# The handover between two layers: residual tiles in a pool of their own, and a piece of a weight moved behind them

## The chip, the cores and the metric

One NeuronCore of a Trainium2 chip runs the whole program. The metric is the device time of one execution in microseconds (us); lower is better. Most figures below come from a profiled execution, whose span is within a few us of its timed value.

## The reference

The program runs two kinds of layer, each twice, with a residual around each: A, B, A, B.

```python
x = A_x                                                       # [1, 2048, 640], bf16
x = x + _A_ref(_layernorm(x), A_wq, A_wk, A_wv, A_wo, A_beta)
x = x + _B_ref(_layernorm(x), B_mem0, B_Wq, B_Wk, B_Wv, B_Wo, B_seg_len)
x = x + _A_ref(_layernorm(x), A_wq, A_wk, A_wv, A_wo, A_beta)
x = x + _B_ref(_layernorm(x), B_mem0, B_Wq, B_Wk, B_Wv, B_Wo, B_seg_len)
```

A is an attention with a compressive memory over 4 segments of 512 rows (32 heads of 20). It ends with `o @ wo` and the residual. B is a recurrence: 64 segments of 32 rows, each attending to itself and to 8 memory rows that the segment before it produced (32 heads of 128). So B's steps are serial, and each ends with the product by `Wo` (32 heads, each 128 x 640 in bf16, 160 KB).

```python
for s in range(n_seg):                                        # layer B
    h = jnp.concatenate([mem, x[:, s*32:(s+1)*32]], axis=1)
    ...                                                       # q, k, v, masked softmax, o
    o = jnp.einsum('bhte,hed->btd', o, Wo)
    mem = o[:, :M, :].copy()
```

## The kernel before

Layer A works in row blocks of 128. In the last segment its output projection `outp` is deferred: layer B calls it as the list `tail`, between B's first products. Each row block takes two products `a_YP` of 320 columns, VectorE's addition of the residual `a_xr`, a store of the float32 rows, a cast to bf16 on GpSimd into `a_xb`, and a store of that. There is one `a_xb` buffer (pool `so`) and there are two `a_xr` buffers (pool `so2`), so the residual tiles of blocks 2 and 3 can only be loaded when blocks 0 and 1 are through.

```python
def res_load(n, tt, q=nc_raw.sync):
    r0 = n * 512 + tt * 128
    xr = so2.tile([128, D], xdt, name="a_xr")
    q.dma_start(xr[:], x_src[r0:r0 + 128, :])
    xin[tt] = xr

def outp(n, i):
    tt, half = divmod(i, 2)
    if half == 0:
        xin[tt, "o"] = so2.tile([128, D], F32, name="a_xo") if src_is_bf16 else xin[tt]
    xo = xin[tt, "o"]
    hs = slice(320 * half, 320 * half + 320)
    YP = pg.tile([128, 320], F32, name="a_YP", tag="pg")
    for c in range(NCH):
        nc.tensor.matmul(YP[:], lhsT=oT[:, c, 128 * tt:128 * tt + 128], rhs=wvo[:, c, hs], ...)
    nc.vector.tensor_tensor(out=xo[:, hs], in0=YP[:], in1=xin[tt][:, hs], op=ALU.add)
    if half:
        r0 = n * 512 + tt * 128
        nc_raw.sync.dma_start(x_dst[r0:r0 + 128, :], xo[:])
        xb = so.tile([128, D], BF16, name="a_xb")
        nc.gpsimd.tensor_copy(xb[:], xo[:])
        nc_raw.sync.dma_start(xb_dst[r0:r0 + 128, :], xb[:])
        if tt + 2 < 4:
            res_load(n, tt + 2, nc.scalar if n == NS - 1 else nc_raw.sync)
```

Wo fills memory as it comes free: heads 0 to 10 while A still runs, heads 11 to 15 by five loads on ScalarE's queue during B's first products, heads 16 to 31 once A's pools are closed.

```python
wo = [wop.tile([128, NW1 - NEARLY, D], BF16, name="b_wo1")]     # NW1 = 16, NEARLY = 11
# ... cut ...
for kind in ("Q", "K", "V"):
    for b in range(2):
        TailUnit(0, kind, b).run(NCH)                           # b_tail in the trace
        flush()
        h = NEARLY + {"K": 0, "V": 2}.get(kind, NW1) + b
        if h < NW1:
            nc.scalar.dma_start(wo[0][:, h - NEARLY, :], wo_src[:, h, :])
for Wt, dst in ((W.wq, QT), (W.wk, KT)):
    for b in range(2):
        # ... cut: one more such load ...
        tail(2)                                                 # two a_YP products of A
        # ... cut: b_first, placed by ScalarE and GpSimd ...
tail(100)
tails_to_seg(0)
outer.close()                                                   # A's pools end here
wop2 = ctx.enter_context(tc.tile_pool(name="b_wo2", bufs=1, side="right", reuse_waits="tile"))
wo.append(wop2.tile([128, 32 - NW1, D], BF16, name="b_wo2"))
for a, b in ((NW1, 24), (24, 32)):
    nc_raw.sync.dma_start(wo[1][:, a - NW1:b - NW1, :], wo_src[:, a:b, :])
```

A scheduler then orders the instructions of each engine. A load waits until the last user of the memory that it takes is done.

Of the kernel before, what the change touches and what calls it, by code (L numbers as in the profile page):

```python
# [18 lines left out]
F32 = mybir.dt.float32  # L19
BF16 = mybir.dt.bfloat16  # L20
# [3 lines left out]
PSUM = bass.MemoryType.PSUM  # L24

S_TOK = 2048
NW1 = 16
EARLY = [(tag, h0, n, at) for tag, h0, n in (("a_phiks", 0, 1), ("a_MZ32", 1, 2), ("a_xnT0", 3, 4), ("a_vaug0", 7, 4)) for at in range(n)]
NEARLY = len(EARLY)
ORDER_ENGINES = ("tensor", "scalar", "vector", "gpsimd")  # L30
D = 640
# [169 lines left out]
def layer_A(nc, nc_raw, tc, C, W, A_wv, A_wo, x_src, x_dst, xb_dst, src_is_bf16, general, outer, mem0, wo_src, prep=None, prefetch=()):  # L201

    SC = 1.0 / math.sqrt(20.0)
    NS, NG = 4, 8
    NU = NS * NG
    xdt = BF16 if src_is_bf16 else F32
    with ExitStack() as ctx:
        br = Bridge()
# [32 lines left out]
        def wload(u):  # L241
            if prep and u < NG:
                wts[u] = W.pad[u]
                return
            wt = wk.tile([128, 2, NCH, 128], BF16, name="a_wt")
            for k in range(2):
                nc_raw.sync.dma_start(wt[:, k].rearrange("p c m -> p (c m)"), W.wpad[u % NG][k])
            wts[u] = [wt[:, 0], wt[:, 1]]
# [78 lines left out]
        def run(gctx):  # L327
# [13 lines left out]
            us, xin = {}, {}  # L341
# [15 lines left out]
            def phi_q(u):  # L357
                if u // NG == 0:
                    return
                U = us[u]  # L360
                t1 = wk1.tile([128, 512], BF16, name="a_t1q", tag="t1")
                nc.vector.tensor_scalar(out=t1[:], in0=U.qk[:, 0, :], scalar1=1.0, scalar2=1.0, op0=ALU.add, op1=ALU.max)
                nc.vector.tensor_tensor(out=U.phiq[:], in0=U.phiq[:], in1=t1[:], op=ALU.min)
# [15 lines left out]
            def row_max(u):  # L379

                U = us[u]
                negm = gp.tile([128, 4, 4], F32, name="a_negm")
                for j in range(4):
                    for qc in range(4):
                        N = 128 * (qc + 1)
                        Sx = pss.tile([128, 2, 512], F32, name="a_Sg", tag="pss")
                        nc.tensor.matmul(Sx[:, 0, 0:N], lhsT=U.qk[32 * j:32 * j + 32, 0, 128 * qc:128 * qc + 128],
                                         rhs=U.qk[32 * j:32 * j + 32, 1, 0:N], start=True, stop=False, tile_position=(32 * j, 0))
                        nc.tensor.matmul(Sx[:, 0, N - 128:N], lhsT=C.identb[:], rhs=negu[:], start=False, stop=True)
                        nc.vector.tensor_reduce(out=negm[:, qc, j:j + 1], in_=Sx[:, 0, 0:N], axis=AX.X, op=ALU.max, negate=True)  # L390
                parts = gp.tile([128, 4, 4, 3], BF16, name="a_mparts")
                for i in range(3):
                    nc.vector.tensor_copy(parts[:, :, :, i], negm[:])
                    if i < 2:
                        nc.vector.tensor_tensor(out=negm[:], in0=negm[:], in1=parts[:, :, :, i], op=ALU.subtract)
                mt = pg.tile([12, 4, 128], BF16, name="a_mt", tag="pg")
                for qc in range(4):
                    nc.tensor.transpose(mt[:, qc, :], parts[:, qc].rearrange("p j i -> p (j i)"), C.identb[:])
                ms = wk1.tile([12, 512], BF16, name="a_ms", tag="t1")
                nc.vector.tensor_copy(ms[:], mt[:].rearrange("p q t -> p (q t)"))  # L400
                for j in range(4):
                    nc_raw.sync.dma_start(U.qk[32 * j + 20:32 * j + 23, 0, :], ms[3 * j:3 * j + 3, :])
                    nc_raw.sync.dma_start(U.qk[32 * j + 20:32 * j + 23, 1, :], ones[:])
# [93 lines left out]
            def o_turn(tt):  # L497
                nc_raw.sync.dma_start(oT[:, :, 128 * tt:128 * tt + 128], Onat[:, tt, :], transpose=True)

            def res_load(n, tt, q=nc_raw.sync):  # L500
                r0 = n * 512 + tt * 128
                xr = so2.tile([128, D], xdt, name="a_xr")
                q.dma_start(xr[:], x_src[r0:r0 + 128, :])
                xin[tt] = xr

            def outp(n, i):
                tt, half = divmod(i, 2)
                if half == 0:
                    xin[tt, "o"] = so2.tile([128, D], F32, name="a_xo") if src_is_bf16 else xin[tt]
                xo = xin[tt, "o"]  # L510
                hs = slice(320 * half, 320 * half + 320)
                YP = pg.tile([128, 320], F32, name="a_YP", tag="pg")
                for c in range(NCH):
                    nc.tensor.matmul(YP[:], lhsT=oT[:, c, 128 * tt:128 * tt + 128], rhs=wvo[:, c, hs], start=(c == 0), stop=(c == NCH - 1))
# [4 lines that stand above are left out]
                    xb = so.tile([128, D], BF16, name="a_xb")  # L519
                    nc.gpsimd.tensor_copy(xb[:], xo[:])  # L520
                    nc_raw.sync.dma_start(xb_dst[r0:r0 + 128, :], xb[:])
                    if tt + 2 < 4:
                        res_load(n, tt + 2, nc.scalar if n == NS - 1 else nc_raw.sync)

            ln = {}

# [85 lines left out]
            for u in range(NU + 1):  # L612
                more = u + 1 < NU
                if u + 2 < NU:
                    wload(u + 2)
                if pre and u % 2:
                    pre.pop(0)()
                if fill_pads and u + 2 < NG:
                    fill_pads(nc, u + 2)
                for slot in range(6):  # L620
                    if u < NU:
                        score(u, slot)
                    if slot == 0 and more:
                        proj(u + 1, 0)
                    if slot == 1 and u >= 1:
                        pvmm(u - 1, 1)
                        norm(u - 1)
                    if slot == 2 and more:
                        proj(u + 1, 1)
                        phi_q(u + 1)  # L630
                    if slot == 4 and u < NU:
                        pvmm(u, 0)
                        if more:
                            phi_k(u + 1)
                    if slot == 5 and u < NU:
                        nummm(u)
                        memory(u)
                    extras(u, slot)
                if general and more:
                    row_max(u + 1)  # L640
            br.tail = [lambda i=i: outp(NS - 1, i) for i in range(8)]

        with ExitStack() as gctx:
            run(gctx)
# [24 lines left out]
def layer_B(nc, nc_raw, tc, C, W, br, outer, wo_src, x_src, xb_src, x_dst, general, nsteps=64, out_bf16=False):  # L669
# [4 lines left out]
    with ExitStack() as ctx:  # L674
# [5 lines left out]
        wop = ctx.enter_context(tc.tile_pool(name="b_wo", bufs=1, reuse_waits="tile"))  # L680
        wo = [wop.tile([128, NW1 - NEARLY, D], BF16, name="b_wo1")]
        pp = ctx.enter_context(tc.tile_pool(name="b_ps", bufs=3, reuse_waits="tile", space=PSUM))

        def wo_of(h):
            for t, h0, n in br.wo:
                if h0 <= h < h0 + n:
                    return t[:, h - h0]
            return wo[0][:, h - NEARLY] if h < NW1 else wo[1][:, h - NW1]

        def ps_tile(shape, dtype, name):  # L690
            return pp.tile(shape, dtype, name=name, tag="ps")
# [43 lines left out]
        def heads(t):  # L735
            return t[:].rearrange("p (h c) -> p h c", h=32)
# [94 lines left out]
        def flush():  # L831
            while done:
                done.pop(0)()

        def tails_to_seg(s):
            T, i = divmod(s, 4)
            nc.gpsimd.tensor_copy(heads(QT[s])[:, :, 32:40], QTt[T][:, :, 8 * i:8 * i + 8])
# [67 lines left out]
        for kind in ("Q", "K", "V"):  # L905
            for b in range(2):
                TailUnit(0, kind, b).run(NCH)
# [6 lines that stand above are left out]
                h = NEARLY + 4 + (b if Wt is W.wq else NW1)  # L914
                if h < NW1:
                    nc.scalar.dma_start(wo[0][:, h - NEARLY, :], wo_src[:, h, :])
# [3 lines left out]
                place(("act", "pool")[b], turn(ps[:]), b, heads(dst[0]), 0, 24, 0)  # L920
        tail(100)
        tails_to_seg(0)
        outer.close()
        wop2 = ctx.enter_context(tc.tile_pool(name="b_wo2", bufs=1, side="right", reuse_waits="tile"))
        wo.append(wop2.tile([128, 32 - NW1, D], BF16, name="b_wo2"))
        for a, b in ((NW1, 24), (24, 32)):
            nc_raw.sync.dma_start(wo[1][:, a - NW1:b - NW1, :], wo_src[:, a:b, :])
        po = ctx.enter_context(tc.tile_pool(name="b_po", bufs=1, reuse_waits="tile", space=PSUM))
        pot = ctx.enter_context(tc.tile_pool(name="b_pot", bufs=2, reuse_waits="tile", space=PSUM))

# [374 lines left out]
```

## Time and profile before

| | before |
|---|---|
| time, median of 4 runs (range) | 2270.47 us (2269.4 to 2272.89) |
| span of the profiled run | 2272.9 us |
| TensorE busy | 2156.6 us, 95% |
| first handover, idle of TensorE in it | 58.31 us, 11.45 us |
| second handover, idle of TensorE in it | 61.80 us, 11.63 us |

The unit for everything that follows is the length of a handover: from TensorE's first `b_tail` matmul, when all of A's products but the deferred `a_YP` are out, to its first `b_Qa` matmul of B's third step. Both ends are read from TensorE's timeline. The table of stretches then gives the work inside, here for the two handovers of the kernel before (columns: the stretch and its length, then busy time and count of TensorE, its weight loads, VectorE, ScalarE, GpSimd; granted clock, DMA share, GB/s):

```profile
288.64:346.95 58.31, 46.86 (x955) 23.68 (x956) 28.08 (x64) 10.56 (x29) 19.57 (x44) 0.89 0.47 123
...
1408.20:1470.00 61.80, 50.17 (x959) 24.57 (x960) 27.67 (x64) 10.46 (x29) 19.84 (x44) 0.82 0.43 121
```

Length minus TensorE's busy time is its idle time. TensorE's work is the same in both handovers, so the difference in busy time, 50.17 against 46.86, is clock: 0.82 against 0.89.

### The profile page before, as it was taken

To read this page: it belongs to the slowest core of one execution; us is meant where nothing else is said; L and a number is where in the kernel's file an instruction comes from. 1 tells how busy PE (TensorE), PEld (TensorE's weight loads), DVE (VectorE), ACT (ScalarE), POOL (GpSimd) and SP (SyncE) were. 2 spreads that over 40 slices of the span, in tenths; PEclk is the share of its full clock that TensorE was granted. 3 is DMA by queue.
4 is the path that set the end of the run, shared out by engine and by line. 5 is a ranking of instruction groups with operands and counts; after the bars stand their busy time and mean duration, and the time that the engine had idled before them with its cause. 6 is when DMAs were issued, how large, how long until landed. Compare 5 with 4: busy or idle time off the path is not lost.

```text
span 2272.9 us, 122154 instructions
## 1 busy us (share of the span) xinstructions
PE 2156.6 (95%) x54486; PEld 1213.7 (53%) x54548; DVE 1632.6 (72%) x3998; ACT 908.6 (40%) x2111; POOL 1023.7 (45%) x2475
## 2 busy tenths in 40 slices
PE   6998889999999999999979999799999999999997
PEld 3444445555555555555544444455555555555554
DVE  5787646777777677777668887477777777777775
ACT  5776723332323323333357766233333233333322
POOL 3454434444444444444423545344444444444442
PEclk9999989999999999999989999899999999999999
DMA  6677841101110101000144665310101110010000
GB/s 159 162 177 176 225 124 23 24 21 28 22 23 21 24 22 24 23 23 19 28 112 123 151 167 137 117 24 18 21 19 20 19 22 19 20 24 19 17 13 14
DMA packets 150233, 137.78 MB, mean 61 GB/s; under 512 B 76080, under 2 KB 139584, under 8 KB 147776
## 3 DMA queue, kind: packets, MB, share of 16 engines
q1 hardware_dynamic: 145504, 124.30, 22.2%
q8 instruction: 428, 7.01, 1.3%
q10 hardware_dynamic: 4192, 5.57, 0.9%
q14 instruction: 109, 0.89, 0.1%
HBM read 89.17 MB, written 26.21 MB: 51 GB/s over the span
## 4 chain that ended last, share of the span: by engine, by line
PE 81%; DVE 7%; DMA 5%; ACT 3%; issue 2%; POOL 1%; SPq 1%; DVEq 0%; ACTq 0%; POOLq 0%
PE b_V L87 13%; PE b_OPS L87 13%; PE b_tail L87 10%; PE b_Qa L87 6%; PE b_Kb L87 6%; PE b_Ka L87 6%; PE b_Qb L87 6%; PE b_SP L87 5%; PE b_OTL L87 4%; PE b_OPSd L87 3%; PE a_PP L87 3%; ACT a_PT L87 2%; PE a_S L87 2%; PE a_VP L87 1%; PE a_pv L87 1%
## 5 line engine op out<-in xcount | busy, mean ns | idle before, releaser
L87 PEld LDWEIGHTS <-b_hT 128*32 128x32 bf16 x15120 | 376.1, 96 | 311.4 <-DVE b_hT L87 69.4
L87 ACT ACTIVATE b_PT<-b_SP 128x224 bf16<-128x224 f32 x256 | 92.2, 360 | 764.2 <-PE b_SP L87 742.5
L87 PE MATMUL b_V<-b_wv,b_hT 128*32 128x512 bf16 x5040 | 358.5, 381 | 0.4 <-issue 0.2
L87 ACT ACTIVATE a_PT<-a_S 128x768 bf16<-128x768 f32 (+1 forms) x384 | 325.9, 883 | 73.1 <-PE a_S L87 51.5
L87 PE MATMUL b_OPS<-b_wo,b_OTsb 128*32 128x320 bf16 x5376 | 258.9, 302 | 8.1 <-DVE b_OTsb L87 5.1
L87 PEld LDWEIGHTS <-b_OTsb 128*32 128x32 bf16 x8192 | 202.0, 97 | 96.3 <-DVE b_OTsb L87 48.2
L87 POOL CAST b_QT<-b_TQ 128x384 bf16<-128x384 f32 x254 | 140.1, 551 | 223.2 <-DVE b_TQ L87 223.2
L87 ACT CAST b_OTsb<-b_OTL 128x320 bf16<-128x320 f32 x384 | 151.2, 427 | 208.2 <-PE b_OTL L87 189.6
L87 POOL TENSOR_TENSOR b_PT<-b_PT,b_R 128x64 bf16<-128x64 bf16 x256 | 105.2, 411 | 215.6 <-ACT b_R L87 198.6
L87 POOL CAST b_KT<-b_TQ 128x384 bf16<-128x384 f32 x254 | 142.4, 561 | 131.6 <-DVE b_TQ L87 128.0
L87 PE MATMUL b_Qa<-b_wq,b_hT 128*32 128x512 bf16 x2520 | 183.6, 384 | 5.0 <-DVE b_hT L87 5.0
L87 PE MATMUL b_Kb<-b_wk,b_hT 128*32 128x512 bf16 x2520 | 183.0, 380 | 0.0
L87 PE MATMUL b_Ka<-b_wk,b_hT 128*32 128x512 bf16 x2520 | 182.9, 383 | 0.0
L87 POOL TENSOR_SCALAR_AFFINE_SELECT a_PT<-a_PT 128x256 bf16<-128x256 bf16 x256 | 109.0, 429 | 157.5 <-ACT a_PT L87 155.3
L87 DVE STREAM_TRANSPOSE b_TM<-b_OPS 128x128 f32<-128x128 f32 x252 | 88.2, 350 | 123.0 <-PE b_OPS L87 119.1
L87 PE MATMUL b_Qb<-b_wq,b_hT 128*32 128x512 bf16 x2520 | 158.4, 379 | 0.0
L87 PE MATMUL a_PP<-a_xnT,a_wt 128*128 128x512 bf16 x505 | 139.3, 388 | 14.6 <-ACT a_phiq L87 5.4
L87 DVE CAST b_Vsb<-b_V 128x512 bf16<-128x512 f32 x128 | 88.5, 692 | 80.0 <-PE b_SP L87 45.6
L87 PE MATMUL b_OPS<-a_wo,b_OTsb 128*32 128x320 bf16 x2816 | 144.6, 301 | 0.0
L87 PE MATMUL a_S<-a_qk 32*128 32x512 bf16 (+3 forms) x1024 | 136.4, 307 | 5.9 <-ACT a_PT L87 4.7
L87 DVE CAST b_OTsb<-b_OTL 128x320 bf16<-128x320 f32 x128 | 62.9, 492 | 100.1 <-PE b_OTL L87 100.1
L87 POOL TENSOR_TENSOR b_Rtot<-b_Rtot,b_R 128x160 bf16<-128x160 bf16 x256 | 126.7, 495 | 0.0
(158 smaller groups left out, 4282.4 us busy)
## 6 DMA issues: line engine op xcount, KB each, us to landing
a_wt<-a_wpad SPq DMA_DIRECT2D x112, 160.0 KB
b_XO<-xres SPq DMA_DIRECT2D x256, 30.0 KB
a_wvo<-in_A_wo_dram SPq DMA_DIRECT2D x8, 800.0 KB
b_wq<-in_B_Wq_dram SPq DMA_DIRECT2D x20, 256.0 KB
b_wk<-in_B_Wk_dram SPq DMA_DIRECT2D x20, 256.0 KB
xres<-a_xo SPq DMA_DIRECT2D x16, 320.0 KB
xres_bf<-a_xb SPq DMA_DIRECT2D x32, 160.0 KB
b_wv<-in_B_Wv_dram SPq DMA_DIRECT2D x20, 256.0 KB
```

The lines of the kernel that those rows point to most:

```text
L87: r = f(*a, **k)
```

## The change

The intent is to let the deferred output projection run without waiting for loads. The residual tiles of row blocks 2 and 3 (and, where the source is bf16, the float32 output tile of block 2) get buffers of their own in a pool `a_tail`, and are loaded ahead of need from SyncE's queue. To make room, Wo's heads 12 to 15 leave the early piece. They are loaded into `a_tail`'s place when it closes, in one 640 KB load ahead of heads 16 to 31.

```diff
-NW1 = 16
+NW1 = 12
@@ res_load, outp
-            def res_load(n, tt, q=nc_raw.sync):
+            def res_load(n, tt):
...
-                q.dma_start(xr[:], x_src[r0:r0 + 128, :])
+                nc_raw.sync.dma_start(xr[:], x_src[r0:r0 + 128, :])
...
-                if half == 0:
+                if half == 0 and (tt, "o") not in xin:
...
-                xo = xin[tt, "o"]
+                xo = xin.pop((tt, "o")) if half else xin[tt, "o"]
...
-                    if tt + 2 < 4:
-                        res_load(n, tt + 2, nc.scalar if n == NS - 1 else nc_raw.sync)
+                    if tt + 2 < 4 and n < NS - 1:
+                        res_load(n, tt + 2)
@@ end of layer A
+            def tail_tiles(pool):
+
+                for tt in (2, 3):
+                    r0 = (NS - 1) * 512 + tt * 128
+                    xin[tt] = pool.tile([128, D], xdt, name=f"a_xr{tt}")
+                    nc_raw.sync.dma_start(xin[tt][:], x_src[r0:r0 + 128, :])
+                if src_is_bf16:
+                    xin[2, "o"] = pool.tile([128, D], F32, name="a_xo2")
+
+            br.tail_tiles = tail_tiles
@@ layer B
+        tail_ctx = ExitStack()
+        br.tail_tiles(tail_ctx.enter_context(tc.tile_pool(name="a_tail", bufs=1, reuse_waits="tile")))
...
+        tail_ctx.close()
         outer.close()
+        wop3 = ctx.enter_context(tc.tile_pool(name="b_wo3", bufs=1, reuse_waits="tile"))
         wop2 = ctx.enter_context(tc.tile_pool(name="b_wo2", bufs=1, side="right", reuse_waits="tile"))
-        wo.append(wop2.tile([128, 32 - NW1, D], BF16, name="b_wo2"))
-        for a, b in ((NW1, 24), (24, 32)):
-            nc_raw.sync.dma_start(wo[1][:, a - NW1:b - NW1, :], wo_src[:, a:b, :])
+        wo.append(wop3.tile([128, 16 - NW1, D], BF16, name="b_wo3"))
+        wo.append(wop2.tile([128, 16, D], BF16, name="b_wo2"))
+        nc_raw.sync.dma_start(wo[1][:], wo_src[:, NW1:16, :])
+        for a, b in ((16, 24), (24, 32)):
+            nc_raw.sync.dma_start(wo[2][:, a - 16:b - 16, :], wo_src[:, a:b, :])
```

## The prediction

> **What bounds the kernel now.** I read the page first, then the table of stretches, then the chain of work that ended last through both handovers, then the timeline of each engine there, last the trace's records of DMA packets, semaphore landings and granted clock. The page:
>
> ```profile
> PE 2156.6 (95%) x54486; PEld 1213.7 (53%) x54548; DVE 1632.6 (72%) x3998; ACT 908.6 (40%) x2111; POOL 1023.7 (45%) x2475
> ```
>
> TensorE is the bound for nearly the whole run, so only TensorE's idle or slow time in the two handovers can be won. The table of stretches compares them (42.00 and 45.60 us) with an ordinary step of B (12.70 us, TensorE never idle):
>
> ```profile
> 288.70:330.70 42.00, 31.86 (x577) 15.91 (x576) 19.87 (x43) 6.13 (x16) 14.04 (x30) 0.91 0.64 167
> 343.40:356.10 12.70, 12.70 (x384) 7.17 (x376) 9.27 (x25) 5.01 (x14) 4.80 (x11) 1.00 0.05 13
> 1408.20:1453.80 45.60, 35.27 (x579) 16.96 (x576) 19.45 (x44) 6.03 (x16) 14.31 (x30) 0.80 0.58 161
> ```
>
> The columns are length, busy time of TensorE, its weight loads, VectorE, ScalarE and GpSimd, granted clock, DMA share, GB/s. TensorE is idle 42.00 - 31.86 = 10.1 us and 45.60 - 35.27 = 10.3 us: 20.4 us together, 0.9% of the run. That caps the idle part of any gain; the reduced clock adds a few us. TensorE's timeline, first two lines in the first handover, last two in the second:
>
> ```profile
> 309.35 1.52 PE L87 MATMUL a_YP<-a_wvo,a_oT 128*128 128x320 bf16 x10 [3.38 <-DVE a_xo L87]
> ...
> 328.65 1.26 PE L87 MATMUL b_OPS<-b_wo,b_OTsb 128*32 128x320 bf16 x16 [2.76 <-DMA b_wo<-in_B_Wo_dram]
> ...
> 1430.64 2.73 PE L87 MATMUL a_YP<-a_wvo,a_oT 128*128 128x320 bf16 x10 [5.12 <-DVE a_xr L87]
> ...
> 1445.68 0.21 PE L87 MATMUL b_OTL<-b_PT,b_Vsb 32*128 32x40 bf16 x1 [3.77 <-issue]
> ```
>
> The change aims at the first and third gaps. VectorE shows their cause, a residual tile or its output buffer:
>
> ```profile
> 308.80 0.89 DVE L87 TENSOR_TENSOR a_xo<-a_YP,a_xr 128x320 f32<-128x320 f32 x2 [4.65 <-DMA xres<-a_xo]
> ...
> 1430.10 0.89 DVE L87 TENSOR_TENSOR a_xr<-a_YP,a_xr 128x320 f32<-128x320 f32 x2 [6.39 <-DMA a_xr<-xres]
> ```
>
> But the chain of the first handover goes on through something else, the bf16 copies a_xb, which have one buffer, and then through the load of Wo:
>
> ```profile
> 303.58 5.10 DMA xres<-a_xo
> ...
> 315.41 1.77 DMA xres_bf<-a_xb
> ...
> 317.75 10.86 DMA b_wo<-in_B_Wo_dram
> 328.65 1.28 PE b_OPS L87 x12
> ```
>
> GpSimd's timeline shows the serial chain: each cast waits for the previous one's store to land.
>
> ```profile
> 300.05 0.72 POOL L87 CAST a_xb<-a_xo 128x640 bf16<-128x640 f32 x1 [2.69 <-DVE a_xo L87]
> 309.28 0.72 POOL L87 CAST a_xb<-a_xo 128x640 bf16<-128x640 f32 x1 [8.51 <-DVE a_xo L87]
> 311.97 0.72 POOL L87 CAST a_xb<-a_xo 128x640 bf16<-128x640 f32 x1 [1.51 <-DMA xres_bf<-a_xb]
> 314.66 0.72 POOL L87 CAST a_xb<-a_xo 128x640 bf16<-128x640 f32 x1 [1.98 <-DVE b_QT L87]
> ```
>
> The named releasers of lines two and four are misleading: the landing records have the first bf16 store (issued 304.03) landing at 309.14 and the third (issued 312.71) at 314.52. I call the end of the fourth cast C: 315.38 here, 1435.40 in the second handover. GpSimd does its placement of the first K only after C, VectorE's transposes wait on that buffer, and TensorE's scores on those; the 2.56 MB Wo load is issued at C + 1.9.
>
> **What the Trainium skill says.** "DMA: Bandwidth & Descriptors", Anatomy of one DMA, puts a fixed cost of about 2 us on a DMA, most of it the receipt (for the GpSimd path). The trace agrees for SyncE's stores here: an undisturbed 160 KB bf16 store takes 1.8 to 1.9 us. The same page, Queues, rings and completion order, has an engine finish a packet of up to 64 descriptors before it turns to another queue. The trace fits it: in the second handover an instruction fetch, which I would expect near 1439.7 from the matmul count, starts at 1442.95, when the first half of Wo is through. "Runtime: NRT & Kernel Launch", Instruction fetch mechanics, says that each sequencer fetches instructions in 16 KiB blocks by its own DMA; the trace has 428 such packets, one per 255 TensorE instructions, and the 3.77 us gap ends 1.5 us after that one. "TensorE: Matmul & The Clock Gate", What's actually happening, says that the clock halves after an idle window of about 3.4 us. The trace has half clock from 328.3 to 335.1 and from 1444.4 to 1458.1, in multiples of 3.41 us, following gaps of only 2.8 and 3.8 us.
>
> **The change part by part.** No compute instruction is added or removed; the order of TensorE, VectorE and GpSimd work is unchanged.
> (1) ScalarE's queue loses two residual loads and four of its five 160 KB Wo loads per handover. In the first handover its queue moved 1.13 MB between 300 and 307 us, just when the first residual store waited to land (5.1 us instead of about 2).
> (2) The two residual loads move to SyncE, behind A's transposes (their space was the transposes' source) and before most small loads of B. They cost two issues at about 0.37 us, but remove waits in the same queue (about 1 us before 303.58). Net I take the first bf16 store 0.7 us earlier in each handover.
> (3) The first bf16 store then meets less traffic. First handover: issue 303.3, less 480 KB of traffic ahead of it at 270 KB/us, landing about 306.5 instead of 309.14, or 307.3 if the fetch at 305.7 delays one of the 16 engines as it did before (15 of 16 completions came 1.3 us before the last). The other three links run as before at about 2.7 us. C becomes 312.5 to 313.3, that is 2.1 to 2.9 earlier. Second handover: landing about 1424.8 instead of 1427.27; then 1425.5, 1427.5, 1428.2, 1430.2, 1430.9 for cast and landing in turn. C moves from 1435.40 to about 1430.9, 4.5 earlier, because the third tile no longer waits for its load.
> (4) Wo heads 12 to 15 (640 KB) go late, before the other 2.56 MB. At the 350 KB/us of the present load that is 1.8 us of DMA. In the first handover the new load comes before the fourth bf16 store, delaying its landing perhaps 0.3; in the second it comes after it and pushes the last Wo half back 1.8 us.
> First handover, end = landing of the last Wo half = C + 13.2 + 0.3: gain 2.4 less 0.3, about 2.0. The output buffer of the fourth block still waits for the first store, but that is hidden below C. Half clock after the remaining gap stays.
> Second handover: Wo flows from 1432.5, 3.2 MB land after 10.2 + 1.8 us, at 1444.5. Then output matmuls, transpose and additions take 2.1 us, and the next step's first half 4.2 us at half clock: the second Q pass starts at about 1451, now 1458.05. Gain about 7; I take 6.5, since a straggling engine is likely. Sum 8.5 us.
>
> **Rivals.** First, the intended saving: the gaps of 3.38 and 5.12 go, the restarts run at full clock, and all is kept, some 15 us or more. For it: those gaps have no other named cause; against it: the a_xb chain and the Wo load end later than they do. That would be 2253. Second, nothing remains: the late 640 KB and a displaced instruction fetch eat it. In the second handover a fetch is due near C + 3 = 1433.9; if it misses the end of the 640 KB and falls behind the first 1.28 MB, a stall near 4 us and half clock return, costing another 2 us or so; the same fetch in the first handover started just as Wo did and cost 1.17, and may get worse. That would be 2265 to 2269. Third, the gap before Wo becomes short enough to avoid half clock: about 2 us more each, 2257.
>
> **Range and chances.** 2269.9 - 8.5 = 2261.4 us. Both bad fetches give about 2266; both clock escapes about 2257. With a run-to-run spread of 3.5 us in the three runs before, I put eight chances in ten on 2256 to 2267. Two per cent is 45 us, twice all idle time of both handovers, so faster by more is 1%, slower by more 0.5%, within 98.5%.
>
> **What would show it.** Right: the gaps 3.38 and 5.12 before the third pair of a_YP are gone; the four a_xb casts still stand 2.7 us apart and the fourth ends near 313 and 1431; TensorE still waits for b_wo before the first step's last output matmuls in both handovers; B's 12.7 us steps are untouched, so the ends of the handovers carry to the end. Wrong: casts closer together or not on the chain, heads 12 to 15 awaited themselves, an issue gap of 3 us or more remaining at the value matmuls, or B's steps or A's stages changing length.

## The result, and the profile after

The changed kernel took 2266.88 us in the median of 4 runs (2262.4 to 2269.53), the kernel before 2270.47 us (2269.4 to 2272.89) beside it. Ratios here are the mean time of one kernel's runs over the mean of the other's in the same rounds, so they are not quite the ratio of the medians: 0.9981, 95% interval 0.9962 to 0.9999, which is 4.3 us of 2270. Both kernels are correct. The predicted 2261.4 was 5.5 us too low, inside the range by a hair (2266.88 against 2267). In relative terms the forecast was 2261.4 / 2269.9 = 0.9963, and the gain half of that.

The two handovers of the changed kernel, as stretches again:

```profile
288.25:345.80 57.55, 46.61 (x955) 23.59 (x956) 28.18 (x64) 10.36 (x29) 19.56 (x44) 0.87 0.47 125
...
1406.93:1462.80 55.87, 45.97 (x956) 23.63 (x956) 27.89 (x64) 10.46 (x29) 19.62 (x44) 0.89 0.51 134
```

The first handover is 0.8 us shorter (58.31 to 57.55), the second 5.9 us (61.80 to 55.87); idle time fell by 0.5 and 1.7 us, and the rest of the second one's gain is clock, 0.89 against 0.82. TensorE's timeline shows what became of the gaps of 3.38 and 5.12 us (start, duration, what, and in brackets the idle time before it and what ended it):

```profile
305.21 1.53 PE L87 MATMUL a_YP<-a_wvo,a_oT 128*128 128x320 bf16 x10
314.31 0.25 PE L87 MATMUL b_SP<-c_mask,c_identb 128*32 128x160 bf16 x4 [2.71 <-DVE b_TQ L87]
322.56 0.73 PE L87 MATMUL b_OPS<-b_wo,b_OTsb 128*32 128x320 bf16 x16 [1.52 <-DMA b_wo<-in_B_Wo_dram]
327.37 1.26 PE L87 MATMUL b_OPS<-b_wo,b_OTsb 128*32 128x320 bf16 x16 [4.08 <-DMA b_wo<-in_B_Wo_dram]
...
1431.62 0.25 PE L87 MATMUL b_SP<-c_mask,c_identb 128*32 128x160 bf16 x4 [2.59 <-DVE b_TQ L87]
...
1445.17 1.26 PE L87 MATMUL b_OPS<-b_wo,b_OTsb 128*32 128x320 bf16 x16 [4.07 <-DMA b_wo<-in_B_Wo_dram]
```

All four blocks of `a_YP` now run without a wait, as intended. But TensorE, through with them earlier, waits later. In the first handover, up to the end of the wait for Wo, the gaps before were 3.38 + 0.91 + 1.17 + 0.63 + 2.76 = 8.85 us (the second, third and fourth are the scores, an issue gap and the first part of the output product, in the same view). Now they are 2.71 + 1.52 + 4.08 = 8.31 us. In the second they were 5.12 + 3.77 + 0.62 = 9.51 us and are 2.59 + 0.63 + 4.07 = 7.29 us (the 0.63 a wait for `b_OTsb`, in a line left out). The `a_YP` gap became a wait for the first scores and a longer wait for Wo.

What sets both is on GpSimd. Its timeline has the casts into the one `a_xb` buffer:

```profile
299.36 0.72 POOL L87 CAST a_xb<-a_xo 128x640 bf16<-128x640 f32 x1 [2.69 <-DVE a_xo L87]
306.95 0.72 POOL L87 CAST a_xb<-a_xo 128x640 bf16<-128x640 f32 x1 [6.87 <-DMA xres_bf<-a_xb]
309.64 0.72 POOL L87 CAST a_xb<-a_xo 128x640 bf16<-128x640 f32 x1 [1.52 <-DMA xres_bf<-a_xb]
312.34 0.72 POOL L87 CAST a_xb<-a_xo 128x640 bf16<-128x640 f32 x1 [1.97 <-DMA xres_bf<-a_xb]
```

They stand 2.7 us apart, each behind the landing of the store before it, now named by the profile as the releaser. The second cast waits for the first bf16 store, and the chain of work that ended last shows why that store is late. SyncE issues small DMAs back to back from 297.33 on (of which this is the last before the store, that of the float32 rows), the store itself starts at 302.83, and the rest of the chain hangs on it:

```profile
302.37 0.34 SPq L518
...
302.83 3.98 DMA xres_bf<-a_xb
...
307.70 1.80 DMA xres_bf<-a_xb
...
310.39 1.80 DMA xres_bf<-a_xb
...
316.66 10.67 DMA b_wo<-in_B_Wo_dram
```

SyncE's queue shows the last links. After, line 942 is the new 640 KB load and line 944 the two loads of heads 16 to 31:

```profile
311.28 0.41 SPq L942 DMA_DIRECT2D b_wo<-in_B_Wo_dram  x1
313.08 0.32 SPq L521 DMA_DIRECT2D xres_bf<-a_xb  x1
316.22 1.16 SPq L944 DMA_DIRECT2D b_wo<-in_B_Wo_dram  x2
```

Before, the same place in the queue looked so:

```profile
315.41 0.32 SPq L521 DMA_DIRECT2D xres_bf<-a_xb  x1
317.30 1.01 SPq L927 DMA_DIRECT2D b_wo<-in_B_Wo_dram  x2
```

The fourth bf16 store took 317.30 - 315.41 = 1.9 us until the big load could follow it. Now it takes 316.22 - 313.08 = 3.1 us: 1.2 us of what the chain had won is lost again behind the new load.

### The profile page after: what moved, and what is told of

Read it like the earlier page. It is cut to its first block, busy times and chain, and to the rows that moved or that the text cites. A ratio compares the mean times of both kernels' runs of the same rounds, so it can differ in the third digit from the quotient of the medians.

```text
span 2267.7 us, 122151 instructions
## 1 busy us (share of the span) xinstructions
PE 2154.5 (95%) x54486; PEld 1216.0 (54%) x54548; DVE 1633.9 (72%) x3998; ACT 908.6 (40%) x2111; POOL 1023.4 (45%) x2475
## 3 DMA queue, kind: packets, MB, share of 16 engines
q1 hardware_dynamic: 147136, 126.60, 22.5%
## 4 chain that ended last, share of the span: by engine, by line
PE 82%; DVE 6%; DMA 5%; ACT 3%; issue 2%; POOL 1%; SPq 1%; ACTq 0%; POOLq 0%; DVEq 0%
PE b_V L87 13%; PE b_OPS L87 12%; PE b_tail L87 10%; PE b_Qa L87 6%; PE b_Kb L87 6%; PE b_Ka L87 6%; PE b_Qb L87 6%; PE b_SP L87 5%; PE a_PP L87 4%; PE b_OTL L87 4%; PE b_OPSd L87 3%; PE a_S L87 2%; ACT a_PT L87 2%; PE a_pv L87 2%; PE a_VP L87 2%
```

## The experiments

The theory after this reading had three parts. First, the serial chain of bf16 copies and stores (end of the fourth cast: C) sets when the last Wo load is issued and so the end of the handover. Second, the residual tiles' early load is what shortens the chain, while the Wo part only makes room. Third, in the first handover the new 640 KB load, ahead of the fourth store in SyncE's queue, delays it. A rival held throughout: differences of a few us between two profiles are luck of the clock.

Each run was timed over five rounds beside the kernel before; e1 to e4 share one chip and its runs of before, so do e5 to e8 and again e9 and e10. The table has for each the ratio and, from its profile, the lengths of the handovers h1 and h2, TensorE's idle time in both together, the time at half clock in both together (from the clock records), C counted from the first `b_tail`, and the same for the issue of the first 1.28 MB load of heads 16 to 31 (in e8 and e10 of its first piece).

| kernel | ratio [95%] | h1, h2 us | idle | half clock | C, first / second | issue of the big load |
|---|---|---|---|---|---|---|
| before (first profile) | 1 | 58.3, 61.8 | 23.1 | 34.9 | 26.7 / 27.2 | 28.7 / 29.1 |
| e6 before again | 0.9997 [0.9979, 1.0016] | 56.8, 58.0 | 23.1 | 23.3 | 25.5 / 25.9 | 27.4 / 27.8 |
| changed (first profile) | 0.9981 [0.9962, 0.9999] | 57.6, 55.9 | 20.8 | 27.7 | 24.8 / 23.4 | 28.0 / 25.4 |
| e1 changed again | 0.9980 [0.9967, 0.9993] | 57.2, 57.4 | 18.0 | 33.6 | 24.8 / 24.1 | 27.8 / 26.1 |
| e2 Wo part alone | 0.9988 [0.9973, 1.0003] | 53.1, 56.7 | 17.6 | 22.8 | 24.7 / 24.3 | 26.7 / 26.3 |
| e5 Wo part alone again | 0.9973 [0.9954, 0.9993] | 55.4, 58.5 | 18.2 | 32.2 | 24.0 / 24.3 | 25.9 / 26.3 |
| e4 640 KB from ScalarE's queue | 0.9990 [0.9974, 1.0005] | 58.2, 55.0 | 18.4 | 30.8 | 25.5 / 24.1 | 28.9 / 26.1 |
| e8 before, late Wo in 8 loads | 0.9982 [0.9963, 1.0001] | 58.1, 55.5 | 20.6 | 20.8 | 26.7 / 27.3 | 28.6 / 29.1 |
| e7 Wo part, two copy buffers | 0.9970 [0.9953, 0.9987] | 54.0, 56.9 | 19.3 | 21.2 | 22.1 / 25.1 | 24.1 / 27.1 |
| e3 changed, two copy buffers | 0.9966 [0.9950, 0.9983] | 53.5, 52.4 | 15.3 | 20.3 | 20.9 / 20.1 | 22.5 / 22.0 |
| e9 the same again | 0.9973 [0.9952, 0.9994] | 53.0, 50.5 | 14.3 | 16.0 | 20.8 / 20.1 | 22.4 / 22.0 |
| e10 the same, late Wo in 8 loads | 0.9963 [0.9943, 0.9982] | 52.1, 50.7 | 11.2 | 20.8 | 21.0 / 20.2 | 22.8 / 22.6 |

Read this table first by its four pairs of equal kernels. For the kernel before, idle time repeats to 0.1 us, while the half clock differs by 12 us and with it the handovers together by 5.3 us. In the other pairs idle time differs by 0.7 to 2.9 us, the half clock by 4 to 9 us. C differs by up to 1.3 us. So one profile tells C to about a microsecond, idle time to about three, and lengths only to several; the profiles also come from different chips. Nor are idle time and half clock independent where a load ends the stretch. In the first handover of the changed kernel idle time fell from 10.9 to 8.3 us between its two profiles, half clock rose from 15.1 to 18.6 us, and the length stayed (57.6 and 57.2): slower work filled what had been a wait for Wo.

### e1: the changed kernel again

No edit. This settles how much of the first profile repeats.

> The changed kernel once more, unedited, for the spread and a second profile. I measure a handover from TensorE's first b_tail matmul to the first b_Qa matmul of the third step of B; before it is 58.3 and 61.8 us, changed 57.6 and 55.9 us in the first profile, so 6.7 us shorter together, while the clock of the whole kernel showed only about 4 us. If the handovers are what the change moved and the rest is chance in the stages between (half clock in the second A, instruction fetches in B's steps), the two handovers repeat within 1 us and the stages between differ by 1 to 3 us in either direction; median time 2263 to 2268. If the second A really became longer (2.95 us in the first profile), it is as long again.

Measured: 2262.95 us median (2260.01 to 2266.85, 6 runs) against 2265.32 (2263.04 to 2271.63, 11 runs), ratio 0.9980. The gain of about 4.5 us (0.002 x 2265) repeats, and its interval leaves out 1. The sum of the handovers is 114.6 us, against 113.4 in the first profile; one repeated to 0.4 us, the other only to 1.5, where I had expected 1. The second A, 269.1 us in the first profile of the changed kernel against 266.3 before, was 267.4 here and 268.7 in e6, so it did not become longer. In the first handover the big load was again issued 3.1 us after C, in the second 1.9.

### e2 and e5: the Wo part alone

```diff
 (against the kernel before)
-NW1 = 16
+NW1 = 12
+        wop3 = ... "b_wo3"; heads 12 to 15 by one 640 KB load from SyncE, then heads 16 to 31
 (no a_tail pool; residual tiles as before, on ScalarE's queue)
```

> The kernel before with only the Wo part of the change: heads 12 to 15 in a tile of their own, loaded late, residual tiles as before. My theory (the residual part gives all the gain, the Wo part only makes room and costs DMA time): gaps of about 3.4 and 5.1 us before the third pair of a_YP stay within 1.5 us, time 2269 to 2273, no gain. The rival, that taking 640 KB off ScalarE's queue is what freed the first residual store: the first bf16 store lands 2 us or more sooner and 3 us or more of the gain are there without the residual tiles, 2265 to 2267.

Measured: 2262.83 us median (2255.86 to 2267.71), ratio 0.9988, which says little. But the profiled run was its fastest one, with a span of 2254.1 us and h1 of 53.1. I therefore ran it again:

> The Wo part alone once more, unedited. In its first profile the handovers were 53.1 and 56.7 us (before 58.3 and 61.8, changed 57.2 to 57.6 and 55.9 to 57.4), but the median of its times was only as good as the changed kernel's. If the Wo part alone, here one early 640 KB load in place of four 160 KB loads on ScalarE's queue, gives the gain, the handovers repeat within 1.5 us and the casts again end near 24.7 and 22 us after the first b_tail matmul; time 2260 to 2265. If the first profile was a lucky one, the handovers come back to 57 us or more each.

Measured: 2262.6 us (2256.61 to 2266.66) against 2266.83 (2263.33 to 2272.79), ratio 0.9973, span 2262.7 us. The mean of the two ratios, 0.998, is that of the changed kernel. So the second part of my theory falls: as far as these timings and the idle time (17.6 and 18.2 us, against 20.8 and 18.0) can tell, the Wo part alone gives as much as the whole. The handovers did not repeat, 55.4 and 58.5 us against 53.1 and 56.7, with 9 us more of half clock; C did, to 0.7 us. (The "22" and "about 24" us that the expectations of e5 and e7 give for the second handover of this kernel were misread; the trace has C at 24.3 and the load at 26.3.) Its SyncE queue (first run, first handover) shows one reason:

```profile
296.94 0.41 SPq L928 DMA_DIRECT2D b_wo<-in_B_Wo_dram  x1
...
310.48 0.32 SPq L521 DMA_DIRECT2D xres_bf<-a_xb  x1
312.38 1.01 SPq L930 DMA_DIRECT2D b_wo<-in_B_Wo_dram  x2
```

Without `a_tail` in its place the scheduler issues the 640 KB load (line 928) at 296.94, before the first bf16 store, and the big loads follow the fourth store after 1.9 us, not 3.1. The gaps before `a_YP` are only partly gone: 1.01 and 2.81 us in this run, 2.07 and 2.32 us in the second, against 3.38 and 5.12 before (2.83 and 5.07 in e6). What ended these waits is as before: in the first handover the landing of the first float32 store, whose output buffer is needed again, in the second the residual tile. So with four of five Wo loads off ScalarE's queue both came earlier, even without buffers of their own; the addition that waits for them starts 17.3 and 17.5 us after the first `b_tail` in the first handover (20.2 and 18.6 before), and 19.2 us in the second in both runs (21.9 and 20.6 before). That it is less traffic that does this fits, but is not tested apart.

The opposite half, the residual tiles alone with NW1 = 16, could not be tried. The pool needs 5 KB per partition where the build reports 1.69 KB left, so that kernel does not build. What the residual part gives by itself stays open.

### e4: the 640 KB load from ScalarE's queue

```diff
 (against the changed kernel)
-        nc_raw.sync.dma_start(wo[1][:], wo_src[:, NW1:16, :])
+        nc.scalar.dma_start(wo[1][:], wo_src[:, NW1:16, :])
```

> The changed kernel with heads 12 to 15 loaded from ScalarE's queue. My theory for the shortfall in the first handover (gain 0.8 where I predicted 2.0): SyncE issues this 640 KB load ahead of the fourth bf16 store, which then lands 2.9 us after its issue instead of 1.8, and the big Wo load waits for that landing. On another queue the store lands about 1 us sooner, the first handover is 0.7 to 1.3 us shorter (about 56.5 us), the second unchanged within 0.5 us. The rival (both queues share the same engines, so it makes no difference): the store still takes 2.7 us or more, first handover 57.3 to 57.8.

Measured: 2265.0 us (2258.86 to 2268.02), ratio 0.9990 [0.9974, 1.0005], not distinguishable from before or from the changed kernel. SyncE's queue in the first handover:

```profile
313.70 0.32 SPq L521 DMA_DIRECT2D xres_bf<-a_xb  x1
317.11 1.08 SPq L944 DMA_DIRECT2D b_wo<-in_B_Wo_dram  x2
```

The load was issued on the other queue at 310.96, yet the fourth store still held the big load back for 3.4 us. So it is not the order in SyncE's queue that costs. Where the 640 KB load was out of the way when the store ran (e2), the same step took 1.9 us. That a 640 KB load in flight slows the store whichever queue it came from fits all of these; through what, no run here tells.

### e3 and e9: a second bf16 copy buffer

```diff
 (against the changed kernel)
-                    xb = so.tile([128, D], BF16, name="a_xb")
+                    xb = xin[tt, "b"] if (tt, "b") in xin and n == NS - 1 else so.tile([128, D], BF16, name="a_xb")
+                xin[1, "b"] = xin[3, "b"] = pool.tile([128, D], BF16, name="a_xb1")   # in a_tail
```

This is the direct test of the chain: blocks 1 and 3 copy into a buffer of their own, so a cast waits for the store before the last.

> The changed kernel with a second buffer for the bf16 copies of the last four blocks (blocks 1 and 3 in a tile of the tail pool). My theory (the chain of copies, each waiting for the store before it, sets when Wo may be loaded and when the first keys are placed): the fourth cast ends 3.5 to 4.7 us sooner than 313.1 and 1430.4 us, counted from the first b_tail matmul 24.8 and 23.4 us now to about 20.5 and 19.5; Wo is issued 3 to 4.5 us sooner; each handover 3 to 5 us shorter, together 6 to 9, time 2256 to 2261. The rival, that the Wo load itself and its DMA traffic bound the handover: it is issued sooner but lands less than 1.5 us sooner, time 2263 to 2267.

Measured: 2258.41 us (2254.41 to 2264.15) against 2265.32, ratio 0.9966, 7.7 us. GpSimd's casts in the first handover, whose first `b_tail` is at 287.22:

```profile
297.98 0.72 POOL L87 CAST a_xb<-a_xo 128x640 bf16<-128x640 f32 x1 [2.69 <-DVE a_xo L87]
300.69 0.72 POOL L87 CAST a_xb<-a_xo 128x640 bf16<-128x640 f32 x1 [2.00 <-DMA a_xr<-in_A_x_dram]
306.03 0.72 POOL L87 CAST a_xb<-a_xo 128x640 bf16<-128x640 f32 x1 [3.39 <-DMA xres_bf<-a_xb]
307.41 0.72 POOL L87 CAST a_xb<-a_xo 128x640 bf16<-128x640 f32 x1 [0.65 <-DVE b_TQ L87]
```

The first three stand where VectorE's additions and the first store put them, and C is 20.9 us after the first `b_tail` instead of 24.8. The first big load is issued 22.5 us after it instead of 28.0. (In this handover the scheduler also put it ahead of the 640 KB load, which went out at 310.16, so more than the buffer moved; in the second handover the order stayed, and the issue still came 3.4 us earlier, 22.0 instead of 25.4.) The waits for the first scores are gone from the list of long gaps. TensorE's remaining gaps over 1.1 us up to the end of the wait for Wo are these, two in each handover:

```profile
316.75 0.18 PE L87 MATMUL b_OTL<-b_PT,b_Vtb 32*128 32x16 bf16 x1 [3.14 <-issue]
322.40 1.26 PE L87 MATMUL b_OPS<-b_wo,b_OTsb 128*32 128x320 bf16 x16 [1.21 <-DMA b_wo<-in_B_Wo_dram]
...
1429.40 0.19 PE L87 MATMUL b_OTL<-b_PT,b_Vsb 32*128 32x40 bf16 x1 [2.26 <-issue]
1436.31 1.26 PE L87 MATMUL b_OPS<-b_wo,b_OTsb 128*32 128x320 bf16 x16 [2.77 <-DMA b_wo<-in_B_Wo_dram]
```

A new wait has come: the issue gap, which the changed kernel had lost, is back, since the due instruction fetch falls into the Wo load again. As e2 had shown that one profile can be lucky, I repeated this kernel on another chip:

> The changed kernel with the second bf16 copy buffer, a second time, to see whether its gain and its short handovers repeat. Theory (the serial chain of bf16 copies sets when the last Wo load is issued): both handovers again 51 to 55 us in the profile, sum 104 to 109, against 113 to 115 for the changed kernel; ratio to the kernel before 0.995 to 0.998. Rival (the first run was clock luck, as the first profile of the Wo part alone was): sum of the handovers 111 or more, ratio 0.998 to 1.000.

Measured: 2265.3 us (2261.12 to 2270.24, 6 runs) against 2274.28 (2266.7 to 2279.57, 11 runs), ratio 0.9973. The handovers sum to 103.4 us, below what I expected, with C and issue within 0.1 us of the first run. The chain theory holds: against the two profiles of the changed kernel C, the issue of the big load and both handovers moved the way the theory says, each by 3 us or more (handovers together 113.4 and 114.6 to 105.9 and 103.4 us, idle time 20.8 and 18.0 to 15.3 and 14.3), and they did so twice. By timing alone, two buffers against one is not settled, as the intervals overlap.

### e7: two copy buffers without the residual tiles' pool

```diff
 (against the Wo part alone)
-                    xb = so.tile([128, D], BF16, name="a_xb")
+                    xb = so.tile([128, D], BF16, name="a_xb", tag=f"a_xb{tt % 2}" if n == NS - 1 and tt % 2 else "a_xb")
```

> The Wo part alone, and a second buffer for the bf16 copies of A's last row blocks; residual tiles still loaded late, from ScalarE's queue. If the chain of copies sets when Wo may go, and the residual tiles' own buffers are not needed for it: the big Wo load is issued 2 us or more earlier than in the Wo part alone (26.6 and about 24 us after the first b_tail matmul), handovers together 3 to 6 us shorter than there (109.8), time 2256 to 2260. If the late residual tiles bound it instead, as the gap of 2.8 us in the second handover suggests: the copies are held by the additions, less than 2 us together, 2260 to 2264.

Measured: 2261.52 us (2255.16 to 2263.18) against 2266.83, ratio 0.9970. C is 22.1 us after the start in the first handover but 25.1 in the second, where e3 had 20.1. Now the late residual tiles bind. GpSimd's third cast in the second handover waits for the addition, not for a store:

```profile
1421.01 0.72 POOL L87 CAST a_xb<-a_xr 128x640 bf16<-128x640 f32 x1 [6.09 <-DVE a_xr L87]
```

and so does TensorE, whose gap of 4.38 us before the `a_YP` at 1420.54 was ended by VectorE's additions into `a_xr`.

So the residual tiles' own pool shows no gain while the one copy buffer sets the end, and becomes needed once that is removed: idle time 19.3 us here, in one profile, against 15.3 and 14.3 with both. In the timing the two are level.

### e6: the kernel before again

No edit, as a null test and to see how its profile repeats.

> The kernel before, unedited, for a second profile of its handovers and the spread of its times. If the handovers are set by program order and DMA, 58.3 and 61.8 us repeat within 1.5 us; if they hang on chance (where a clock window or an instruction fetch falls), they differ by 3 us or more, and differences of that size between kernels with one profile each prove nothing. Ratio 1.000 within 0.0015.

Measured: 2266.82 us (2261.24 to 2272.56), ratio 0.9997 [0.9979, 1.0016], as it should be. Its span was 2262.6 us against 2272.9 in the first profile; the second handover took 58.0 us, not 61.8, at 13.0 us of half clock, not 22.6. The baseline profile from which I predicted had drawn a long second handover. The issue gap of 3.77 us was there in both.

### e8 and e10: the late Wo in smaller loads

```diff
 (e8 against the kernel before; e10 the same against e3, for heads 16 to 31)
-        for a, b in ((NW1, 24), (24, 32)):
+        for a, b in [(h, h + 2) for h in range(NW1, 32, 2)]:
```

This tests the instruction fetch: if it stands behind long pieces of the Wo load, shorter pieces should let it through.

> The kernel before with the late Wo load cut from two loads of eight heads into eight of two. My theory for the gap named issue in the value matmuls (a 16 KB instruction fetch waits until an engine has finished its 64 descriptors of a Wo load): with 16 descriptors per engine and load the fetch starts within 1 us, the gap in the second handover falls from 3.8 to 1.6 us or less, and half clock there from 13.7 to about 7 us; second handover 3 to 6 us shorter, time 2261 to 2264. The rival, plain bandwidth (the fetch shares engines with 2.56 MB however it is cut): gap 3 us or more, no change in time.

Measured for e8: 2264.3 us (2257.81 to 2269.02), ratio 0.9982 [0.9963, 1.0001]. The issue gap of the second handover, 3.77 us in both profiles of the kernel before, is

```profile
1439.16 0.19 PE L87 MATMUL b_OTL<-b_PT,b_Vsb 32*128 32x40 bf16 x1 [1.44 <-issue]
```

with everything ahead of it unchanged (C at 27.3). The 16 KB instruction packet of that place started 32.3 us after the first `b_tail` instead of 34.8 and 34.5, that is, over 2 us earlier, and the gap is 2.3 us shorter. The traces hold a wider check. Nineteen gaps of TensorE named issue and over 0.5 us lie in the handovers of the twelve profiles, from 0.63 to 3.91 us long. Each of them ended 1.1 to 1.5 us after such a packet had ended. A rival that would end so regularly is not in sight, so I take these gaps for waits for instructions.

> The changed kernel with the second bf16 copy buffer, and heads 16 to 31 of Wo loaded in eight loads of two heads, not two of eight. Theory of the delayed instruction fetch: the issue gaps of 3.1 and 2.3 us that the two-copies kernel showed in its handovers shrink to 1.5 us or less; with the chain theory both gains add: sum of the handovers 102 to 107 us, ratio to the kernel before 0.994 to 0.997, the fastest kernel of all. Rival (the gap's length is only one more idle stretch beside the wait for Wo, so the later wait grows by what the gap loses): sum unchanged at 104 to 109, ratio as two copies alone, 0.995 to 0.998; then the pieces are not worth their six more issues.

Measured for e10: 2263.72 us (2259.88 to 2266.04) against 2274.28, ratio 0.9963, the best of all kernels and so the version that I would keep, though its interval overlaps that of e3 and e9. The sum of the handovers, 102.8 us, is within the expectation, and idle time is the least, 11.2 us. But the reason that I had given is a miss. In TensorE's timeline the issue gaps are

```profile
317.23 0.18 PE L87 MATMUL b_OTL<-b_PT,b_Vtb 32*128 32x16 bf16 x1 [1.83 <-issue]
...
1430.99 0.21 PE L87 MATMUL b_OTL<-b_PT,b_Vsb 32*128 32x40 bf16 x1 [3.01 <-issue]
```

and not 1.5 us or less (3.14 and 2.26 in e3, 2.66 and 3.91 in e9). What went was the wait for Wo: no single one over 0.51 us is left. The output products can now start on each pair of heads when it lands, though e9's second handover, behind its gap of 3.91 us, had no such wait over 0.4 us either. The sum of the handovers is that of e9 within 0.7 us, so what the pieces add is not shown. These issue gaps too ended 1.3 us after an instruction packet did. In the second handover that packet started at 1428.38, 0.4 us after the gap had begun; why so late, with small loads, stays open.

## Why the prediction was right or wrong

**What bounds the handover: right.** The chain of copies, then the last Wo load, was the path. The gaps before `a_YP` went, and the time saved there was mostly not kept; four casts stayed 2.7 us apart; TensorE still waits for `b_wo` before the first step's last output products in both handovers; B's steps are the same work. e3 and e9 show the chain by cutting it.

**The first bf16 store and C: right in direction; in size only against the first profile.** In the first handover the store was issued 14.6 us after the first `b_tail` instead of 15.4 (0.8 earlier, 0.7 predicted), and C moved from 26.7 to 24.8 us, 1.9 against 2.1 to 2.9. In the second it moved from 27.2 to 23.4, 3.8 against 4.5. But against e6 and e1 the moves are 0.7 and 1.8 us: the first profile of before stood about 1.3 us late at this point in both handovers. By the repeats, C gained well under half of what was predicted.

**The delay by the new load: mis-sized.** This is the step that failed in the first handover. The prediction put "perhaps 0.3" on the new load's cost to the fourth store. Both profiles of the changed kernel show the big load 3.1 to 3.2 us after C instead of 1.9, thus about 1.2 us. With C 1.9 earlier that leaves 0.7 us for the issue of the big load (28.7 to 28.0) and 0.8 us for the handover, not 2.0. With the repeats, 27.4 (e6) and 27.8 (e1), nothing is left. The mechanism named for it, the place ahead of the store, also needs a correction: e4 shows that another queue does not help.

**The second handover: the steps came out, the yardstick did not.** The second Q pass of B's second step began at 1450.89, predicted about 1451; relative to the start of the handover that is 5.9 us earlier than before, 6.5 predicted. (That 1451 itself was met so closely is partly luck: it was reckoned on the times of the old run, and this handover began 1.3 us sooner.) The issue gap was gone, as the main line of the prediction had it. But the 6.5 was counted against a profile with 22.6 us of half clock there. In e6 the same kernel had 13.0 us and a handover 3.8 us shorter. The mean h2 is 59.9 us for the two profiles of before and 56.6 us for the two of the changed kernel: 3.3 us, half of the term. The failing step is treating the half clock after a gap as part of the baseline's fixed cost, when it was one draw.

**The sum.** By the means of two profiles each, the handovers gained 0.2 + 3.3 = 3.5 us. Idle time gained 23.1 - 19.4 = 3.7 us, but half of that in the first handover, which got only 0.2 us shorter: more half clock took its place. The timings say 4.3 and 4.5. All of these are about half of the predicted 8.5, but loosely: the 95% intervals of the timings reach from 0.2 to 8.6 and from 1.6 to 7.5 us. That the time still fell inside the range, by 0.12 us, is luck as much as merit. What a profile shows outside the handovers differs by several us between runs of one kernel (the stretch before the first handover was 288.6 and 285.0 us in the two profiles of before), so nothing of the rest can be put down to the change.

**The rivals.** That all of both gaps would be kept is refuted. That nothing remains is refuted by the timing (both intervals leave out 1, the first barely), though the time fell into the range given for it, 2265 to 2269; its named cause, a fetch stall, was not in the first profile of the changed kernel, and e1 has one of 1.95 us in the second handover. The escape from half clock did not happen: 27.7 and 33.6 us of it remained in the two handovers together.

**What I had not asked.** Which half of the change does the work. The Wo part, which I had taken for the cost, gives about the whole gain alone (e2, e5). The residual part shows in idle time only with a second copy buffer (e3, e9 against e7), and in the timing not at all.

## What to carry to other kernels

Removing a wait on the bound engine gains only what the next chain allows: before sizing it, follow the chain that releases the engine's next wait too, and look for a single buffer whose every reuse waits for a store to land. When gains are a few microseconds, take each kernel's profile twice, the baseline's first of all: equal kernels differed here by up to 2.9 us in idle time and 12 us in time at half clock. An early load may be free in its queue and still delay a small store on which a big transfer waits.

## What the Trainium skill lacked or had wrong

- "TensorE: Matmul & The Clock Gate", What's actually happening, gives half clock "after ≥1 idle window (~3.4µs)". Shorter idle was enough here. In the changed kernel's first handover the clock records fall to half at 323.9 us. In the 3.41 us before that, its timeline has 1.52 us of idle time and the first 0.6 us of the gap of 4.08 us, which began at 323.29. A gap of 2.71 us ending at 314.31 in the same handover was not followed by half clock. The page does say that the window runs freely, which fits the variation between runs: 34.9 and 23.3 us at half clock in the handovers of one kernel. Laid out in the records' windows of 3.41 us, from 20 us after the start, all twelve profiles agree: of the windows at full clock, every one with 2.04 us of idle time or more was followed by half clock, and the idlest one that was not had 2.03. But some were followed by it after only 0.5 us of idle time, in A's stages, so idle time is not all that counts.
- "Runtime: NRT & Kernel Launch", Instruction fetch mechanics, calls the cost of crossing a block boundary "mostly hidden". In a handover with a large load in flight gaps of 0.6 to 3.9 us were not hidden (3.77 us twice in the kernel before): all nineteen ended 1.1 to 1.5 us after a 16 KB instruction packet had ended. What makes the fetch late with small loads (3.01 us in e10) is open.
- No page that I read has a figure for what a 640 KB load in flight adds to a 160 KB store: here about 1.2 us (3.1 instead of 1.9), with another queue no less (3.4).
